# Short outputs as rows through TensorE, silu's slope on ScalarE, and a pool for the spectra products, in a training step of a state-space block with a gated feed-forward layer

## The chip, the cores and the metric

The kernel runs on one core of one Trainium2 chip. The metric is the device time of one execution, in microseconds (us). A core has several engines, each with its own stream of instructions: TensorE (PE in the profile; its weight loads are PEld), VectorE (DVE), ScalarE (ACT), GpSimd (POOL) and SyncE (SP, which here only issues DMA transfers; SPq is its queue). The kernel before took between 934 and 946 us in the median, depending on the group of runs, and in one group its single runs lay between 936.66 and 947.21. So kernels of different groups are compared by their ratio to the kernel before of the same group, or by the length of a stage within one trace.

## The reference, cut to what matters

The reference is a forward pass and its gradient; the outputs are the result and the gradients of the eleven inputs that it depends on. Sizes: L = 2048 positions, D = 512 channels, N = 128 states, F = 1792 hidden units.

```python
xn = layernorm(x)
# A: state-space block, a long convolution by FFT
dt = exp(log_dt)                              # one number per channel: 512
K  = einsum("dn,dnl,dn->dl", C, exp(dt*A*l), dt*B).real
s  = irfft(rfft(xn) * rfft(K)) + xn * Dskip   # Dskip: 512 numbers
# B: feed-forward layer
h  = xn @ w1
g  = silu(silu(h) @ w2)
return x + s * g
# ... and the gradients of x, A, B, C, log_dt, Dskip, w1, w2 for a given grad_out
```

Three parts of the gradient matter here: the gradient of `Dskip` (512 numbers, called ddb in the kernel), the gradient of `log_dt` (512 numbers, ddt), and silu'(h), a factor on every element of the hidden layer's gradient (1792 x 2048), called the slope.

## The kernel before

The kernel interleaves its parts with Python generators, and a scheduler in the compiler places instructions on the engines. It has five stages by time: forward pass, convolution stages (four channel blocks of 128; each does forward and inverse transforms as matmuls), the w2 gradient, the hidden gradient (called the dh stage), and a tail (the last w1-gradient blocks, sixteen tiles of dx, and the parameter gradients of the state-space block).

The gradient of Dskip, once for each channel block. The accumulation leaves one number in each of 128 partitions, and it is stored from there:

```python
ds = C.io.tile([P, T, P], BF16, name="ds_b", tag="ds")
nc.sync.dma_start(ds[:], k.cat_d[:, :, 2, blk])
psd = k.psum1.tile([P, P], F32, name="ps_dsk", tag="psd")
for t in range(T):
    nc.tensor.matmul(out=psd[:], lhsT=ds[:, t, :], rhs=k.xn[:, t, blk], ...)
...scalar_tensor_tensor(out=dd, in0=psd, in1=k.ident, ..., accum_out=dda)
nc.vector.tensor_copy(out=ddb[:], in_=dda[:])                  # 128 partitions x 1
nc.gpsimd.dma_start(k.outs[9][blk].rearrange("(p o) -> p o", o=1), ddb[:])
```

The slope. The forward pass stores silu(h) and tanh(h/2); the backward pass builds the slope from both with two VectorE operations per tile of 128 x 2048 (there are 14):

```python
nc.scalar.activation(out=aT[:, ft, :], in_=pf, func=ACT.Silu)          # forward
nc.scalar.activation(out=th[:, s], in_=pf, func=ACT.Tanh, scale=0.5)
# ... backward, gen_dh, for each tile ft:
nc.vector.tensor_scalar(out=th, in0=th, scalar1=-0.5, scalar2=0.5, ...)
nc.vector.scalar_tensor_tensor(out=th, in0=a, scalar=-1.0, in1=th, op0=ALU.add, op1=ALU.mult)
for tcn in range(4):
    ...   # 4 matmuls into ps_da
    nc.vector.scalar_tensor_tensor(out=k.dhT[:, ft, ls], in0=th[:, ls], scalar=1.0, in1=ps, ...)
# then, for the tile before: DH = transposes of dhT (PE), copied out of PSUM by ScalarE;
# ps_w1 += DH^T xn (16 matmuls), the w1 gradient
```

A small addition on POOL inside the loop that builds the convolution kernel K. It adds Dskip to 32 elements of KF. SP's queue stores KF to K_b right after it, and other transfers stand behind that store in the same queue:

```python
nc.gpsimd.tensor_tensor(out=KF[64*e:64*e+1, 0, :], in0=KF[64*e:64*e+1, 0, :], in1=k.dsk0[...], op=ALU.add)
...
nc.sync.dma_start(K_b[...], KF[...])
```

The end of the parameter gradients, a chain on VectorE (`gen_ssm_final`, run beside the dx tiles; ScalarE only scales two of the outputs).

```python
def emit(out_ap, src, m):
    ob = fin.tile(shp, BF16, name="emit_o", tag="emit_o" + sfx, bufs=2)
    ...                                    # scale into ob
    nc.sync.dma_start(out_ap[bs]..., ob[:])
... # 38 operations on 128 x 512 elements; six results leave through emit
tmul(nc, ddt_b[:], ddt[:], dtb[:])                              # 128 partitions x 4
nc.sync.dma_start(k.outs[8][bs].rearrange("(k p) -> p k", p=P), ddt_b[:])
```

## Time and profile before

Before takes 937.39 us (median; 935.88 to 937.6). Its profiled run has a span of 932.0 us. Stage ends are read from the first and last starts of named matmuls.

| stage of the profiled run | from, to | us |
|---|---|---|
| forward pass | start to last ps_o | 217.7 |
| convolution stages | to first pt_o | 403.5 |
| w2 gradient | to first ps_da | 56.9 |
| dh stage | first to last ps_da | 171.1 |
| tail | last ps_da to end | 82.8 |

The page of before: its first part gives busy time, the second cuts the span into 40 slices of 23.3 us. A digit is the busy share in tenths; PEclk is the clock granted to TensorE, in tenths; GB/s is what the DMA engines moved.

```profile
PE 743.2 (80%) x6870; PEld 488.3 (52%) x6940; DVE 707.4 (76%) x1146; ACT 640.7 (69%) x1174; POOL 95.3 (10%) x147
...
PE   4479899886758887796579668898999797898992
...
PEclk9788999999879999998899979999999898999997
...
GB/s 281 188 135 220 207 255 212 186 238 149 155 66 103 77 230 69 81 125 141 75 81 121 131 178 154 250 210 301 231 258 248 229 255 240 214 239 94 162 84 79
```

No engine is busy throughout. In the slices around 260, 360, 455 and 530 us PE falls to 5 to 7 tenths, in the first three of them with traffic of 66 to 81 GB/s. The table by stretches shows the first of these places. Its columns are the stretch, its length, busy time with instruction count for each of PE, PEld, DVE, ACT and POOL, then PEclk, the DMA share and GB/s:

```profile
247.00:252.00 5.00, 4.95 (x44) 3.02 (x43) 1.85 (x3) 5.00 (x11) 0.69 (x1) 1.00 1.50 113
252.00:256.00 4.00, 3.47 (x63) 2.75 (x61) 3.45 (x7) 3.99 (x10) 0.00 (x0) 1.00 0.91 13
...
260.00:268.00 8.00, 0.48 (x3) 0.30 (x3) 0.40 (x1) 0.52 (x1) 0.00 (x0) 0.67 0.81 59
268.00:272.00 4.00, 3.23 (x20) 2.35 (x21) 1.76 (x4) 2.88 (x5) 0.00 (x0) 0.50 0.57 163
```

At 247 us the Dskip store is issued. Traffic then falls to 13 GB/s, and from 260 to 268 us all engines stand: PE does 0.48 us of work in 8. Afterwards PE runs at half clock. The DMA engines' time is taken (share 0.91 and 0.81), yet few bytes move (13 and 59 GB/s). The view of the tile ddb gives the store itself, with its four issues and the time from issue to landing:

```profile
L728 POOL DMA_DIRECT2D out_dram<-ddb x4: 542/557/689, 247.1 to 520.2; - x4
...
DMA to landing us min/median/max: 15.4/15.4/15.4
```

The waits of PE (line and tile, what released it, us in total, times, longest; "issue" means that the profile names no releaser):

```profile
PE ps_s_3149 L87 <- ACT dftA L74: 12.8, 1, 12.8
PE ps_s_7860 L87 <- ACT KF L74: 9.3, 1, 9.3
...
PE pf_t L619 <- issue: 8.2, 2, 8.0
PE pf_t L619 <- ACT DX L74: 8.0, 1, 8.0
...
PE ps_dsk L721 <- DMA ds_b<-cat_d: 7.1, 3, 6.0
```

The first line is the place at 224 to 237 us. PE's stands after the first, third and fourth Dskip store are the lines with 8.0 (issue), 8.0 (DX) and 9.3 us (KF). In the first ScalarE stood 8.8 us as well, without a named releaser.

In the dh stage VectorE's slope operations are these (view of the tile th_ft; shortest, median and longest in ns):

```profile
L838 DVE TENSOR_SCALAR th_ft<-th_ft x14: 680/685/696, 622.3 to 845.4; 128x2048 bf16<-128x2048 bf16 x14
L839 DVE SCALAR_TENSOR_TENSOR th_ft<-a_ft,th_ft x14: 2278/2292/2293, 623.5 to 846.1; 128x2048 bf16<-128x2048 bf16 x14
```

They cost 14 x (0.685 + 2.292) = 41.7 us of VectorE. In that stage VectorE is busy for 151.0 and PE for 151.0 of 171.1 us. The tail, in three stretches: the last w1 blocks, the dx tiles on PE, and the end after them:

```profile
849.20:861.10 11.90, 9.59 (x69) 5.20 (x70) 2.84 (x6) 6.42 (x8) 11.90 (x21) 1.00 0.55 162
861.10:914.10 53.00, 51.91 (x240) 23.50 (x243) 44.82 (x89) 18.71 (x38) 6.57 (x12) 1.00 0.60 126
914.10:932.00 17.90, 0.40 (x2) 0.00 (x0) 12.78 (x30) 7.63 (x14) 0.00 (x0) 0.61 0.16 59
```

Here PE goes straight on from the last ps_da, and VectorE's parameter chain runs beside the dx tiles.

### The profile page before, as it was taken

The page shows a single profiled execution, that of the slowest core. Times are in us where ns is not written, and L with a number is a line of the kernel's source. Part 1 is how long each engine was busy: PE and PEld are TensorE (multiplying, and loading weights), DVE is VectorE, ACT ScalarE, POOL GpSimd, SP SyncE. Part 2 cuts the span into 40 slices and gives each one's busy share as a digit, 9 for nine tenths or more (in the row PEclk, how much of TensorE's full clock was granted, in tenths as well). Part 3 has the DMA queues.
Part 4 walks back from the last instruction along what each step waited for, and adds up shares of the span by engine and source line. Part 5 has one row for each costly group of instructions (what it writes and reads, how often), then busy time and mean ns, then how long its engine had stood idle before and what let it go on. Part 6 is the DMA issues. An engine that isn't in the chain of part 4 may idle for free. (4 is left out here: it accounts for less than half of the span.)

```text
span 932.0 us, 17458 instructions
## 1 busy us (share of the span) xinstructions
PE 743.2 (80%) x6870; PEld 488.3 (52%) x6940; DVE 707.4 (76%) x1146; ACT 640.7 (69%) x1174; POOL 95.3 (10%) x147
## 2 busy tenths in 40 slices
PE   4479899886758887796579668898999797898992
PEld 1235555554536776684469546564545453544441
DVE  6958899959547988995689238953379898796887
ACT  5998979785858898997699666666635454554144
POOL 4101000304000000021000030010100000006100
PEclk9788999999879999998899979999999898999997
DMA  9436686664953299247934995889898888673562
GB/s 281 188 135 220 207 255 212 186 238 149 155 66 103 77 230 69 81 125 141 75 81 121 131 178 154 250 210 301 231 258 248 229 255 240 214 239 94 162 84 79
DMA packets 194642, 161.97 MB, mean 174 GB/s; under 512 B 132800, under 2 KB 159296, under 8 KB 194560
## 3 DMA queue, kind: packets, MB, share of 16 engines
q1 hardware_dynamic: 189824, 146.43, 61.5%
q0 software_dynamic: 4736, 14.43, 5.5%
q8 instruction: 54, 0.88, 0.4%
q14 instruction: 28, 0.23, 0.1%
HBM read 87.30 MB, written 67.11 MB: 166 GB/s over the span
## 5 line engine op out<-in xcount | busy, mean ns | idle before, releaser
L597 DVE TENSOR_TENSOR ym<-T_97 128x1024 bf16<-128x1024 bf16 x128 | 83.3, 682 | 32.5 <-PE pf_y L636 23.8
L74 ACT CAST Vb<-psV 128x512 bf16<-128x512 f32 x128 | 69.4, 609 | 38.1 <-issue 20.7
L597 DVE TENSOR_TENSOR X<-T_97 128x1024 bf16<-128x1024 bf16 x128 | 81.8, 686 | 14.4 <-PE ps_k L643 14.4
L619 PE MATMUL pf_t<-ident_bfloat_79,X 128*128 128x128 bf16 x1024 | 71.1, 228 | 25.0 <-issue 8.2
L619 PEld LDWEIGHTS <-X 128*128 128x128 bf16 x1024 | 65.6, 103 | 32.0 <-issue 27.5
L74 ACT CAST XTf<-pf_t 128x512 bf16<-128x512 f32 x128 | 67.8, 628 | 1.6 <-PE pf_t L619 1.5
L131 PEld LDWEIGHTS <-prod 128*128 128x128 bf16 x512 | 48.9, 100 | 25.7 <-DVE prod L122 13.8
L678 PE MATMUL ps_h<-XNT,W_127 128*128 128x512 bf16 x213 | 56.9, 407 | 5.9 <-ACT th L682 4.9
L844 PE MATMUL ps_da<-DOT,W2T 128*128 128x512 bf16 x218 | 51.9, 380 | 0.2
L926 PE MATMUL psV<-XT,Gbd 128*128 128x256 bf16 x256 | 42.3, 287 | 11.7 <-ACT Vb L74 5.8
L886 PE MATMUL ps_dx<-W1T,dhT 128*128 128x512 bf16 x220 | 50.6, 379 | 1.1 <-ACT dxn L890 0.9
L692 PE MATMUL ps_o<-W_129,aT 128*128 128x512 bf16 x212 | 50.3, 381 | 1.4 <-ACT th_2090 L696 0.4
L652 POOL TENSOR_TENSOR KF<-KF,dsk_714 1x32 bf16<-1x32 bf16 x16 | 33.3, 2081 | 166.7 <-ACT KF L74 107.4
L926 PEld LDWEIGHTS <-Gbd 128*128 128x128 bf16 x256 | 35.0, 175 | 20.2 <-issue 10.1
L72 DVE COPY dftB<-pt_b 128x1024 bf16<-128x1024 bf16 x24 | 16.5, 687 | 38.1 <-PE pt_b L95 30.1
L87 PEld LDWEIGHTS <-TF 128*128 128x128 bf16 x384 | 26.4, 103 | 31.4 <-issue 21.8
L95 PE MATMUL pt_b<-ident_bfloat_79,dftA 128*128 128x128 bf16 x384 | 30.2, 237 | 15.3 <-ACT dftA L74 7.5
L682 ACT ACTIVATE th<-ps_h 128x512 bf16<-128x512 f32 x56 | 38.0, 685 | 4.2 <-DMA th_d<-th 4.2
L678 PEld LDWEIGHTS <-W_127 128*128 128x128 bf16 x224 | 22.4, 103 | 31.3 <-issue 13.0
L681 ACT ACTIVATE aT<-ps_h 128x512 bf16<-128x512 f32 x56 | 37.9, 681 | 0.2
L643 PEld LDWEIGHTS <-X 128*128 128x128 bf16 x1024 | 35.1, 99 | 5.5 <-issue 2.2
L845 DVE SCALAR_TENSOR_TENSOR dhT<-th_ft,ps_da 128x512 bf16<-128x512 bf16 x56 | 35.2, 679 | 3.0 <-PE ps_da L844 2.9
(1394 smaller groups left out, 1981.2 us busy)
## 6 DMA issues: line engine op xcount, KB each, us to landing
xt_d<-XTf SPq DMA_DIRECT2D x32, 512.0 KB, 2.8
XT<-xt_d SPq DMA_DIRECT2D x32, 512.0 KB, 5.4
YT<-yt_d SPq DMA_DIRECT2D x64, 256.0 KB, 4.0
yt_d<-YTf SPq DMA_DIRECT2D x32, 256.0 KB, 3.4
th_d<-th SPq DMA_DIRECT2D x28, 256.0 KB, 2.3
at_d<-aT SPq DMA_DIRECT2D x4, 1792.0 KB, 6.8
a_ft<-at_d SPq DMA_DIRECT2D x14, 512.0 KB, 6.6
th_ft<-th_d SPq DMA_DIRECT2D x14, 512.0 KB, 6.2
```

The costliest lines, as they stand in the source:

```text
L74: self.nc.scalar.copy(out=out, in_=in_)
L131: nc.tensor.matmul(out=ps[:, gi].rearrange("p a b -> p (a b)"), lhsT=prods[g0 // H][:, ca, cb, g0 % H + gi, :], rhs=W[:, w].rearrange("p a ...
L597: nc.vector.tensor_tensor(out=out.rearrange("p (r h l u) -> p r h l u", h=nh, l=4, u=2), in0=h, in1=l, op=ALU.mult)
L619: nc.tensor.matmul(out=pf[:, qi, m // 2, :], lhsT=X[:, m, q + qi], rhs=k.ident[:], start=(m % 2 == 0), stop=(m % 2 == 1))
L678: nc.tensor.matmul(out=ps[:], lhsT=W1[:, dk, ft * P:(ft + 1) * P], rhs=XNT[:, dk, 4 * tcn:4 * tcn + 4, :], start=(dk == 0), stop=(dk == DK ...
L681: nc.scalar.activation(out=aT[:, ft, :], in_=pf, func=ACT.Silu)
L682: nc.scalar.activation(out=th[:, s], in_=pf, func=ACT.Tanh, scale=0.5)
L692: nc.tensor.matmul(out=pso[:], lhsT=aT[:, ft, tt * P:(tt + 1) * P], rhs=W2[:, ft, :], start=(ft == 0), stop=(ft == FT - 1))
L844: nc.tensor.matmul(out=ps[:], lhsT=W2T[:, dk, rows], rhs=DOT[:, dk, ls], start=(dk == 0), stop=(dk == DK - 1))
L845: nc.vector.scalar_tensor_tensor(out=k.dhT[:, ft, ls], in0=th[:, ls], scalar=1.0, in1=ps[:], op0=ALU.add, op1=ALU.mult)
L886: nc.tensor.matmul(out=ps[:], lhsT=k.dhT[:, ft, t * P:(t + 1) * P], rhs=W1T[:, ft, :], start=(ft == 0), stop=False)
L926: nc.tensor.matmul(out=psV[:, qi].rearrange("p a b -> p (a b)"), lhsT=Gbd[:, :, :, :, 32 * (q_ // 2 % 2) + 4 * c + 2 * (q_ % 2) + q_ // 4] ...
```

## The change

The change has three intents. Short outputs shall leave as contiguous rows and not as one element per partition: TensorE turns them, for Dskip by a matmul with a column of ones, for ddt by a transpose. The slope shall come from ScalarE's own function on stored h. And the spectra products, with the tiles dKs and DXC, shall have a pool of their own, so that they do not share memory with the transforms. Beside these, the chain in the tail takes exp(log_dt) from the forward pass and no longer loads and exponentiates it again.

```diff
-        pr = big.tile([P, 2, 2, H, P], BF16, name="prod", tag="prod", bufs=2)
+        pr = C.pr.tile([P, 2, 2, H, P], BF16, name="prod", tag="prod", bufs=2)
 ...  # dKs and DXC likewise: C.big -> C.pr
-                nc.scalar.activation(out=th[:, s], in_=pf, func=ACT.Tanh, scale=0.5)
-            nc.sync.dma_start(thv[:, f0:f0 + 2, ls], th[:])
+                nc.scalar.copy(out=h_[:, s], in_=pf)
+            nc.sync.dma_start(hv[:, f0:f0 + 2, ls], h_[:])
 ...  # gen_conv_d
-    ...scalar_tensor_tensor(out=dd[:], in0=psd[:], ..., in1=k.ident[:], accum_out=dda[:])
-    ddb = C.io.tile([P, 1], BF16, name="ddb", tag="ddb")
-        nc.gpsimd.dma_start(k.outs[9][blk].rearrange("(p o) -> p o", o=1), ddb[:])
+    nc.vector.tensor_tensor(out=dd[:], in0=psd[:, 0], in1=k.ident[:], op=ALU.mult)
     yield from dft_fwd(k, C, ds[:], DX)
+    nc.tensor.matmul(out=psd[0:1, 1], lhsT=k.ones[:], rhs=dd[:], start=True, stop=True)
+    ddb = C.io.tile([1, P], BF16, name="ddb", tag="ddb")
+    nc.gpsimd.dma_start(k.outs[9][blk].rearrange("(o p) -> o p", o=1), ddb[:])
 ...  # backward
+def silu_slope(k, ft):
+    sl = fa.tile([P, 2048], BF16, name="slope", tag="slope", bufs=3)
+    nc.sync.dma_start(sl[:], k.h_d[ft * P:ft * P + P, :])
+    nc.scalar.activation(out=sl[:], in_=sl[:], func=ACT.Derivative_silu)
 ...  # da(ft): the two VectorE operations go; the last multiply stays
-            nc.vector.scalar_tensor_tensor(out=k.dhT[:, ft, ls], in0=th[:, ls], scalar=1.0, in1=ps[:], ...)
+            nc.vector.tensor_tensor(out=k.dhT[:, ft, ls], in0=sl[:, ls], in1=ps[:], op=ALU.mult)
+        if ft + 2 < FT:
+            silu_slope(k, ft + 2)
 ...  # gen_ssm_final
-        nc.gpsimd.dma_start(ldt[:], k.ins["A_log_dt"][bs].rearrange("(k p) -> p k", p=P))
-    nc.scalar.activation(out=dtb[:], in_=ldt[:], func=ACT.Exp)
+    nc.vector.tensor_copy(out=dtb[:], in_=k.dtN[:, b0:b0 + nb])
 ...
-        nc.sync.dma_start(k.outs[8][bs].rearrange("(k p) -> p k", p=P), ddt_b[:])
+    nc.tensor.transpose(out=pt[0:DK, :], in_=ddt_b[:], identity=k.ident[:])
+    nc.vector.tensor_copy(out=row[:], in_=pt[0:DK, :])
+    nc.sync.dma_start(k.outs[8][bs].rearrange("(k p) -> k p", p=P), row[:])
```

More of the change, by code (lines that the diff above doesn't have):

```diff
@@ L178 @@
     k.at_d = dr.tile([F, L], BF16, name="at_d")
-    k.th_d = dr.tile([F, L], BF16, name="th_d")
+    k.h_d = dr.tile([F, L], BF16, name="h_d")
     k.ident = make_identity(nc, k.const)
@@ L218 @@
         st_fp.close()
-    C = KCtx(); C.big = st_c.enter_context(pool("cbig", "right")); C.io = st_c.enter_context(pool("cio", "right"))
+    C = KCtx(); C.big = st_c.enter_context(pool("cbig", "right")); C.pr = st_c.enter_context(pool("cprod", "right")); C.io = st_c.enter_context(pool("cio", "right"))
     def conv(b):
@@ L488, in ssm_magnitudes @@
         nc.tensor.matmul(out=pd[:, b:b + 1], lhsT=k.dtb[0:1, b * P:(b + 1) * P], rhs=k.ones[0:1, :], start=True, stop=True)
-    dtN = tp.tile([P, NB], F32, name="dtN")
+    dtN = k.dtN = k.const.tile([P, NB], F32, name="dtN")
     nc.vector.tensor_copy(out=dtN[:], in_=pd[:])
@@ L666, in gen_ffn_fwd @@
     W1, XNT, W2 = k.W1, k.XNT, k.W2
-    thv = k.th_d[:].rearrange("(f p) l -> p f l", p=P)
+    hv = k.h_d[:].rearrange("(f p) l -> p f l", p=P)
     atv = k.at_d[:].rearrange("(f p) l -> p f l", p=P)
@@ L672, in gen_ffn_fwd @@
         for f0 in range(0, FT, 2):
-            th = fp.tile([P, 2, 512], BF16, name="th", tag="th", bufs=2)
+            h_ = fp.tile([P, 2, 512], BF16, name="h_", tag="h_", bufs=2)
             for s in range(2):
@@ L717, in gen_conv_d @@
     C.DX = DX = C.big.tile([P, 2, 16, P], BF16, name="DX", tag="DX")
-    psd = k.psum1.tile([P, P], F32, name="ps_dsk", tag="psd")
+    psd = k.psum1.tile([P, 2, P], F32, name="ps_dsk", tag="psd")
     for t in range(T):
-        nc.tensor.matmul(out=psd[:], lhsT=ds[:, t, :], rhs=k.xn[:, t, blk], start=(t == 0), stop=(t == T - 1))
-    dd = C.io.tile([P, P], F32, name="dd", tag="dd")
-    dda = C.io.tile([P, 1], F32, name="dda", tag="dda")
-    nc.vector.scalar_tensor_tensor(out=dd[:], in0=psd[:], scalar=1.0, in1=k.ident[:], op0=ALU.mult, op1=ALU.mult, accum_out=dda[:])
-    ddb = C.io.tile([P, 1], BF16, name="ddb", tag="ddb")
-    nc.vector.tensor_copy(out=ddb[:], in_=dda[:])
-    with nc.allow_non_contiguous_dma(reason="256 B"):
-        nc.gpsimd.dma_start(k.outs[9][blk].rearrange("(p o) -> p o", o=1), ddb[:])
-    yield from dft_fwd(k, C, ds[:], DX)
-    dKs = C.big.tile([P, T, P], BF16, name="dKs", tag="so")
+        nc.tensor.matmul(out=psd[:, 0], lhsT=ds[:, t, :], rhs=k.xn[:, t, blk], start=(t == 0), stop=(t == T - 1))
+    dd = C.io.tile([P, P], BF16, name="dd", tag="dd")
+    nc.vector.tensor_tensor(out=dd[:], in0=psd[:, 0], in1=k.ident[:], op=ALU.mult)
+    yield from dft_fwd(k, C, ds[:], DX)
+    nc.tensor.matmul(out=psd[0:1, 1], lhsT=k.ones[:], rhs=dd[:], start=True, stop=True)
+    ddb = C.io.tile([1, P], BF16, name="ddb", tag="ddb")
+    nc.vector.tensor_copy(out=ddb[:], in_=psd[0:1, 1])
+    nc.gpsimd.dma_start(k.outs[9][blk].rearrange("(o p) -> o p", o=1), ddb[:])
+    dKs = C.pr.tile([P, T, P], BF16, name="dKs", tag="so")
     yield from dft_inv_mul(k, C, C.UX[:], DX[:], dKs, conj_a=True, four=False)
@@ L760, in gen_conv_dx @@
 def gen_conv_dx(k, C, b):
-    DXC = C.big.tile([P, T, P], BF16, name="DXC", tag="so")
+    DXC = C.pr.tile([P, T, P], BF16, name="DXC", tag="so")
     yield from dft_inv_mul(k, C, C.KX[:], C.DX[:], DXC, conj_a=True, four=False)
@@ L797, in gen_dw2 @@
         yield
-def da_loads(k, ft):
+def silu_slope(k, ft):
     nc, fa = k.nc, k.fa
-    rows = slice(ft * P, ft * P + P)
-    a = fa.tile([P, 2048], BF16, name="a_ft", tag="a_ft", bufs=2)
-    nc.sync.dma_start(a[:], k.at_d[rows, :])
-    th = fa.tile([P, 2048], BF16, name="th_ft", tag="th_ft", bufs=2)
-    nc.sync.dma_start(th[:], k.th_d[rows, :])
-    k.aths[ft] = a, th
+    sl = fa.tile([P, 2048], BF16, name="slope", tag="slope", bufs=3)
+    nc.sync.dma_start(sl[:], k.h_d[ft * P:ft * P + P, :])
+    nc.scalar.activation(out=sl[:], in_=sl[:], func=ACT.Derivative_silu)
+    k.slopes[ft] = sl
 def dh_operands(k):
     nc, fa = k.nc, k.fa
-    k.aths = {}
+    k.slopes = {}
     for ft in range(2):
-        da_loads(k, ft)
+        silu_slope(k, ft)
     k.W2T = fa.tile([P, k.DK, k.F], BF16, name="W2T")
@@ L834, in da @@
         rows = slice(ft * P, ft * P + P)
-        if ft not in k.aths:
-            da_loads(k, ft)
-        a, th = k.aths[ft]
-        nc.vector.tensor_scalar(out=th[:], in0=th[:], scalar1=-0.5, scalar2=0.5, op0=ALU.mult, op1=ALU.add)
-        nc.vector.scalar_tensor_tensor(out=th[:], in0=a[:], scalar=-1.0, in1=th[:], op0=ALU.add, op1=ALU.mult)
+        sl = k.slopes.pop(ft)
         for tcn in range(4):
@@ L844, in da @@
                 nc.tensor.matmul(out=ps[:], lhsT=W2T[:, dk, rows], rhs=DOT[:, dk, ls], start=(dk == 0), stop=(dk == DK - 1))
-            nc.vector.scalar_tensor_tensor(out=k.dhT[:, ft, ls], in0=th[:, ls], scalar=1.0, in1=ps[:], op0=ALU.add, op1=ALU.mult)
+            nc.vector.tensor_tensor(out=k.dhT[:, ft, ls], in0=sl[:, ls], in1=ps[:], op=ALU.mult)
+        if ft + 2 < FT:
+            silu_slope(k, ft + 2)
     da(0)
@@ L961, in gen_ssm_final @@
         nc.gpsimd.dma_start(Pm[nm][:], k.ins[key][bs].rearrange("(k p) n -> p k n", p=P))
-    ldt = fin.tile([P, DK], BF16, name="n_ldt" + sfx)
-    with nc.allow_non_contiguous_dma(reason="1 KB"):
-        nc.gpsimd.dma_start(ldt[:], k.ins["A_log_dt"][bs].rearrange("(k p) -> p k", p=P))
     dtb = fin.tile([P, DK], BF16, name="n_dtb" + sfx)
-    nc.scalar.activation(out=dtb[:], in_=ldt[:], func=ACT.Exp)
+    nc.vector.tensor_copy(out=dtb[:], in_=k.dtN[:, b0:b0 + nb])
     ndt = fin.tile([P, DK], BF16, name="n_ndt" + sfx)
@@ L1024, in gen_ssm_final @@
     tmul(nc, ddt_b[:], ddt[:], dtb[:])
-    with nc.allow_non_contiguous_dma(reason="1 KB"):
-        nc.sync.dma_start(k.outs[8][bs].rearrange("(k p) -> p k", p=P), ddt_b[:])
+    pt = k.psumT.tile([P, P], BF16, name="pt_dt", tag="pt")
+    nc.tensor.transpose(out=pt[0:DK, :], in_=ddt_b[:], identity=k.ident[:])
+    row = fin.tile([DK, P], BF16, name="ddt_r" + sfx)
+    nc.vector.tensor_copy(out=row[:], in_=pt[0:DK, :])
+    nc.sync.dma_start(k.outs[8][bs].rearrange("(k p) -> k p", p=P), row[:])
 _INS = ['A_u', 'A_A_re', 'A_A_im', 'A_B_re', 'A_B_im', 'A_C_re', 'A_C_im', 'A_log_dt', 'A_Dskip', 'B_x', 'B_w1', 'B_w2', 'grad_out']
```

## The prediction

> **What bounds it now.** No single engine: the page gives PE 80%, DVE 76%, ACT 69% of 932 us. Time is lost where all stand still.
>
> 1. *Two-byte stores.* Four times (247, 348, 438, 520 us) the Dskip gradient leaves as 128 packets of 2 bytes, 15.4 us to landing each (DMA view). In the table by stretches traffic falls from about 240 to 6-30 GB/s for 12-15 us after each. Other stores queue behind, XTf/YTf buffers stay occupied, and PE, DVE and ACT all stop: 8, 2, 7 and 9 us, with the clock at 0.5 for about 4 us after the long ones: 30 us together. The fifth (893 us) is the 15.3 us DMA entry in the chain of waits, but costs DVE only 4 us of waits. The Trainium skill (DMA: Bandwidth & Descriptors, Rules for kernel authors) says a non-contiguous last dimension becomes one descriptor per element; the trace agrees.
> 2. At 224-237 us PE waits 12.8 us, behind an ACT wait for the last cat_d store, whose memory dftA reuses.
> 3. In the dh stage (680-850 us) PE and DVE are both near full; PE visibly waits only about 14 us.
>
> **What the change does.**
>
> - *Rows:* remove the stalls of point 1: 30 us, less about 7 given back to the next limit (256-byte loads; POOL's KF add, which holds K_b stores): -23 (-12 to -30).
> - *Pool:* in the instruction order dftA no longer waits for a DMA, but ps_dsk needs ds_b, which comes behind the same POOL add (11.6 us): 0 (+/-4).
> - *Forward:* 56 Tanh (0.68 us) become copies (0.6-0.69 us): 0.
> - *Slope:* DVE loses 14 x (0.68 + 2.29) = 42 us; the last multiply stays at 0.68. ACT gains 14 x 1.9 = 27 us (estimate from the skill, ScalarE: Activation LUTs, What ACT_TABLE_LOAD costs: 186 ns + 0.833 ns per element). PE was almost full: -5; the first two slopes delay ACT's DOT copies: +2.
> - *Tail, the cost:* turning ddt puts a transpose on PE. In the changed order it stands directly after the last ps_da, before the last two dW1 blocks and all 16 dx tiles, and waits for DVE's whole parameter-gradient chain: loads about 6 us, then 31 operations of 0.6 us, 18 us. PE stands about 27 us. Then 11.6 us of dW1, about 2 us of slow clock and 16 x 3.24 = 52 us of dx follow in series. From the last ps_da to the end: 82 us before, about 98 after, although the log_dt load (DVE waits 9.1 us) and the 2-byte store are gone: +16 (+10 to +20).
>
> Sum -10: **928 us, range 911 to 944.** Faster by over 2%: 0.21; within 2%: 0.76; slower: 0.03.
>
> **What would show it.** ddb stores landing in about 2 us with no all-engine gap after; conv stages (220-560 us) some 20 us shorter. DVE busy down 40 us, ACT up 25. A PE wait of 20-30 us before the transpose pt_dt, for DVE's ddt_b, with PE near 0 in that slice; dx tiles then paced by PE at 3.24 us, not DVE at 2.5.
>
> **What would make it wrong.** The conv stage may be held by POOL's add, starved by a busier DVE: half the gain. ACT's slopes, in order before PSUM copies, may stall PE more than I count. The parameter chain may finish sooner, the tail cheaper by 5-8 us; with all 30 us of the stores the result would be faster by over 2%.

The DMA view has 32 packets of the first store's queue at 248 to 249 us in before, and 32 for the row at 258 to 259 us in after: the trace does not show one packet per element there. For ddt's store it does (528 packets of the queue between 893 and 896 us, for 512 elements).

## The result, and the profile after

After takes 931.77 us (median; 931.23 to 934.74) against 937.39. The ratio is 0.995, with a 95% interval of 0.9927 to 0.9973: half a per cent faster. Executions over 1.5% slower than the fastest of the same kernel are left out of the means. Ratios in this document are the mean time of one kernel's fast runs over that of the other's in the same rounds, so they are not quite the ratio of the medians quoted. By stage, in the profiled runs:

| stage | before | after | difference | predicted |
|---|---|---|---|---|
| forward pass | 217.7 | 216.8 | -0.9 | 0 |
| convolution stages | 403.5 | 378.9 | -24.6 | -23 |
| w2 gradient | 56.9 | 55.5 | -1.4 | +2 |
| dh stage | 171.1 | 173.4 | +2.3 | -5 |
| tail | 82.8 | 105.4 | +22.6 | +16 |

These two runs differ by 2.0 us in all, the medians by 5.6 us; the stages of one trace are not better than a few us against each other. (The first stage alone took 216.8 to 221.3 us in kernels that share its code.) The page of after:

```profile
PE 736.0 (79%) x6878; PEld 484.8 (52%) x6945; DVE 670.7 (72%) x1116; ACT 666.4 (72%) x1187; POOL 98.4 (11%) x146
...
PE   4469989887488887986798788999798879840997
...
PEclk9889999999698999998999899999899999985999
...
GB/s 279 191 135 225 208 254 219 187 235 143 158 99 103 113 176 63 116 94 180 83 56 227 200 135 238 200 307 215 201 219 200 222 193 208 148 100 127 23 125 45
```

VectorE lost 36.7 us of work and ScalarE gained 25.7, about as forecast. The convolution slices of PE (the 10th to the 25th) hold 7 to 9 tenths but for two: a 4 at 232 to 256 us, which is a wait told below, and a 6. In the tail a slice with PE at 0 has appeared; the slice before it has 4. Nothing like it is in before.

The store of the Dskip gradient, and the stretches after its first issue at 257 us:

```profile
L729 POOL DMA_DIRECT2D out_dram<-ddb x4: 522/523/642, 257.0 to 515.1; - x4
...
DMA to landing us min/median/max: 1.7/2.3/2.6
```

```profile
257.00:262.00 5.00, 4.72 (x81) 4.25 (x78) 4.98 (x8) 4.96 (x11) 0.64 (x1) 1.00 0.42 94
...
266.00:270.00 4.00, 1.83 (x20) 0.97 (x18) 4.00 (x6) 4.00 (x10) 0.00 (x0) 1.00 0.20 68
270.00:278.00 8.00, 6.94 (x105) 6.30 (x104) 8.00 (x14) 6.37 (x14) 0.00 (x0) 1.00 0.30 100
```

The same store lands in 2.3 us, and the standstill is gone: PE does 6.94 us of work in the 8 us from 270, at full clock. (From 266 to 270 it has 1.83 of 4 us, but VectorE and ScalarE are busy throughout.) The waits of PE after:

```profile
PE pt_dt L1020 <- DVE ddt_b L60: 33.5, 1, 33.5
PE ps_dsk L721 <- DMA ds_b<-cat_d: 21.7, 3, 15.2
...
PE ps_w L851 <- ACT DH L74: 10.5, 7, 5.5
```

The first line is the tail's loss: one wait of 33.5 us before the new transpose. The second is the loss that the pool's removal of the dftA wait turned into: PE now waits for ds_b. The third belongs to the dh stage. The tail in stretches:

```profile
824.60:858.50 33.90, 0.38 (x2) 0.00 (x0) 25.92 (x41) 1.25 (x2) 13.94 (x25) 0.55 0.50 143
858.50:871.30 12.80, 10.72 (x68) 6.08 (x71) 0.21 (x1) 4.93 (x6) 0.00 (x0) 0.86 0.00 0
871.30:923.10 51.80, 51.59 (x241) 23.50 (x243) 32.80 (x75) 23.67 (x47) 2.88 (x5) 1.00 0.25 82
923.10:930.00 6.90, 0.36 (x2) 0.00 (x0) 2.62 (x6) 1.50 (x3) 0.00 (x0) 0.77 0.10 38
```

A stretch of 33.9 us with 0.38 us of PE work is new. The w1 blocks take 0.9 us more, the dx tiles 1.2 us less. The end after the last dx matmul is 11.0 us shorter, since the chain is over by then. Together: 33.9 + 0.9 - 1.2 - 11.0 = 22.6. The Trainium skill (TensorE: Matmul & The Clock Gate, Step-by-step: what each phase is for) says that only weight loads are pulled ahead and that the "MATMULs themselves stay in program order". The trace agrees: nothing of the ready w1 blocks ran in the 33.5 us. What the wait consists of shows in VectorE's timeline (start, length, instruction, and in brackets the idle time before it):

```profile
827.74 0.69 DVE L60 TENSOR_TENSOR dBr<-n_Br,n_dtb 128x512 f32<-128x512 bf16 x1 [2.03 <-DMA n_Br<-in_A_B_re_dram]
...
847.43 0.69 DVE L60 TENSOR_TENSOR emit_o<-CSi,n_ndt 128x512 bf16<-128x512 f32 x1 [4.76 <-DMA out_dram<-emit_o]
...
856.85 0.69 DVE L1014 TENSOR_TENSOR ddt_acc<-ddt_acc,cm 128x512 f32<-128x512 f32 x1
857.57 0.69 DVE L1016 TENSOR_REDUCE ddt<-ddt_acc 128x4 f32<-128x512 f32 x1
858.29 0.16 DVE L60 TENSOR_TENSOR ddt_b<-ddt,n_dtb 128x4 bf16<-128x4 f32 x1
```

From dBr to ddt_b are 39 operations, 38 steps from start to start. (858.29 - 827.74 - 4.76) / 38 = 0.68 us each; an operation that needs the one just before it starts 0.72 us after it. In the middle VectorE stands 4.76 us for an output buffer whose store has not landed.

ScalarE's timeline at the beginning of the dh stage, and the load of the slope (view of its tile):

```profile
663.57 1.91 ACT L805 ACTIVATE slope<-slope 128x2048 bf16<-128x2048 bf16 x1 [2.08 <-DMA slope<-h_d]
665.38 1.91 ACT L74 COPY DH<-pt_f 128x1024 bf16<-128x1024 bf16 x2
667.21 1.91 ACT L805 ACTIVATE slope<-slope 128x2048 bf16<-128x2048 bf16 x1
```

```profile
L804 SPq DMA_DIRECT2D slope<-h_d x14: 320/380/1181, 588.4 to 793.8; - x14
L805 ACT ACTIVATE slope<-slope x14: 1909/1914/1968, 596.4 to 800.7; 128x2048 bf16<-128x2048 bf16 x14
...
  DMA slope<-h_d: 7.5, 5
```

The activation takes 1.91 us, which the Trainium skill (ScalarE: Activation LUTs, What ACT_TABLE_LOAD costs) gives as 186 ns + 0.833 ns per element, an estimate of 1.89 us for 2048. But ScalarE stood 2.08 us for its load, then did the slope, and only then the copy DH that PE needed: this is PE's single wait of 5.5 us (2.08 for the load, 1.91 for the slope, the rest for the copy). In all ScalarE waited 7.5 us in five places for these loads.

### The profile page after: what moved, and what is told of

It reads as the page before. It is cut to its first block, busy times and chain, and to the rows that moved or that the text cites. A ratio compares the mean times of both kernels' runs of the same rounds, so it can differ in the third digit from the quotient of the medians.

```text
span 930.0 us, 17456 instructions
## 1 busy us (share of the span) xinstructions
PE 736.0 (79%) x6878; PEld 484.8 (52%) x6945; DVE 670.7 (72%) x1116; ACT 666.4 (72%) x1187; POOL 98.4 (11%) x146
## 5 line engine op out<-in xcount | busy, mean ns | idle before, releaser
L60 DVE TENSOR_TENSOR T<-Vb,YT 128x1024 bf16<-128x1024 bf16 (+1 forms) x96 | 78.1, 863 | 44.6 <-ACT Vb L74 43.5
L597 DVE TENSOR_TENSOR ym<-T 128x1024 bf16<-128x1024 bf16 x128 | 83.6, 682 | 27.7 <-PE pf_y L636 19.3
L597 DVE TENSOR_TENSOR X<-T 128x1024 bf16<-128x1024 bf16 x128 | 81.9, 686 | 5.9 <-PE ps_k L643 5.8
L619 PE MATMUL pf_t<-ident_bfloat,X 128*128 128x128 bf16 x1024 | 69.4, 225 | 10.8 <-ACT h__2430 L682 2.9
L131 PE MATMUL ps_i<-WI,prod 128*128 128x256 bf16 x512 | 64.5, 278 | 15.1 <-DVE prod L122 11.8
L840 DVE TENSOR_TENSOR dhT<-slope,ps_da 128x512 bf16<-128x512 bf16 x56 | 36.6, 683 | 46.0 <-PE ps_da L839 45.8
L74 ACT CAST dftA<-ps_i 128x512 bf16<-128x512 f32 x88 | 48.0, 613 | 22.6 <-PE ps_i L131 22.1
L851 PE MATMUL ps_w<-xn,DH 128*128 128x512 bf16 x211 | 54.9, 405 | 11.2 <-ACT DH L74 10.5
L678 PE MATMUL ps_h<-XNT,W 128*128 128x512 bf16 x213 | 55.4, 397 | 7.2 <-ACT h__633 L682 2.1
L692 PE MATMUL ps_o<-W,aT 128*128 128x512 bf16 x212 | 50.0, 379 | 1.5 <-ACT th L696 0.4
L793 PE MATMUL ps_w<-DO_all,A_ft 128*128 128x512 bf16 x214 | 50.1, 379 | 0.7 <-ACT Vb L74 0.2
L74 ACT CAST dftA<-ps_s 128x512 bf16<-128x512 f32 x92 | 48.6, 670 | 0.1
L95 PE MATMUL pt_b<-ident_bfloat,dftA 128*128 128x128 bf16 x384 | 31.6, 242 | 14.2 <-ACT dftA L74 7.6
```

The costliest lines, as they stand in the source:

```text
L60: nc.vector.tensor_tensor(out=out, in0=a, in1=b, op=ALU.mult)
L74: self.nc.scalar.copy(out=out, in_=in_)
L131: nc.tensor.matmul(out=ps[:, gi].rearrange("p a b -> p (a b)"), lhsT=prods[g0 // H][:, ca, cb, g0 % H + gi, :], rhs=W[:, w].rearrange("p a ...
L597: nc.vector.tensor_tensor(out=out.rearrange("p (r h l u) -> p r h l u", h=nh, l=4, u=2), in0=h, in1=l, op=ALU.mult)
L619: nc.tensor.matmul(out=pf[:, qi, m // 2, :], lhsT=X[:, m, q + qi], rhs=k.ident[:], start=(m % 2 == 0), stop=(m % 2 == 1))
L678: nc.tensor.matmul(out=ps[:], lhsT=W1[:, dk, ft * P:(ft + 1) * P], rhs=XNT[:, dk, 4 * tcn:4 * tcn + 4, :], start=(dk == 0), stop=(dk == DK ...
```

## The experiments

Sixteen kernels ran in five groups. Two of them give wrong results; all the others were correct. Each is told with its ratio to the kernel before of its group; after's own ratio is 0.995.

### a_late: the transpose after the dx tiles

```diff
-    (the transpose, the copy and the store of ddt in gen_ssm_final)
+    (the same three, after interleave([gen_dx(k), gst], [1, 3]); ddt_b lies in the constant pool)
```

> The kernel after, with only the PE transpose of ddt moved: it is emitted after the last dx tile, nothing else changes. Theory (the time lost in the tail is PE standing in program order before the transpose, 33.5 us in the trace of after): PE starts the last dW1 blocks at once after the last ps_da, the stretch from the last ps_da to the end falls from 105.0 to about 75 to 82 us, and the whole to about 904 us (900 to 910). Rival (the tail is bound by VectorE's longer chain and the dx adds behind it, so that PE's wait is only where it shows): the tail stays within 8 us of 105 and the time above 922 us.

Measured: 908.3 us, ratio 0.9611 (0.9549 to 0.9673). In this group before took 946.12, more than in the first, so the expected 904 is missed by 4 us while the ratio is 3.4% below after's. The tail is 77.7 us:

```profile
831.10:843.00 11.90, 9.59 (x69) 5.22 (x70) 8.73 (x14) 4.93 (x6) 11.86 (x21) 1.00 0.55 155
843.00:896.00 53.00, 51.72 (x240) 23.52 (x243) 43.06 (x92) 20.70 (x42) 4.99 (x9) 1.00 0.42 128
896.00:908.80 12.80, 0.55 (x3) 0.08 (x1) 8.13 (x19) 4.97 (x10) 0.00 (x0) 0.62 0.16 58
```

The first two stretches are as long as those of before. What follows: one matmul's place in PE's order cost 105.4 - 77.7 = 27.7 us. The rest of the change in the tail (a row, no second load of log_dt) gains 82.8 - 77.7 = 5.1 us, as far as single traces tell. The rival, that VectorE's chain bound the tail, falls.

### a_ddtcol: ddt as a column again

```diff
-    nc.tensor.transpose(...); copy; nc.sync.dma_start(k.outs[8][bs]...("(k p) -> k p"), row[:])
+    nc.sync.dma_start(k.outs[8][bs].rearrange("(k p) -> p k", p=P), ddt_b[:])
```

> The kernel after, with ddt leaving as a column of 2-byte elements again, without a transpose; the rest as after. Theory: PE no longer waits for ddt, so this gains most of what the moved transpose gains: about 908 us (902 to 915); the 2-byte store itself lands in about 15 us but delays little, since few loads are then outstanding. Rival (the 2-byte store at the end cost as much as the transpose does): 920 us or more.

Measured: 911.92 us, ratio 0.9659 (0.9606 to 0.9712); tail 85.2 us. As expected in size. But "delays little" was wrong: PE waited 10.4 us for a DXC_s load, and then ran at a clock of 0.51. That load was issued from POOL's queue at 872.6 us, 1.6 us after this store, and landed only after 21.3 us. In before the chain ends later: the same store goes out at 893.2 us, after the last DXC_s load (887.7), and PE did not wait for it. A column of single elements cost 85.2 - 77.7 = 7.5 us even here; the transpose in its bad place cost more.

### a_ddbcol: only the Dskip gradient as a column again

```diff
-    nc.vector.tensor_tensor(out=dd, in0=psd[:, 0], in1=k.ident); ones matmul; row store
+    scalar_tensor_tensor with accum_out; [P, 1] store, as in the kernel before
```

> The kernel after, with only the Dskip gradient leaving as a column of 2-byte elements again, four times. Theory (these four stores made the standstills in the convolution stages): the all-engine gaps after each store come back, the stretch to the first ps_da grows by about 23 us and the time is about 955 us (950 to 962). Rival (the pool of their own for the products gave the gain in the convolution stages): below 938 us.

Measured: 955.71 us, ratio 1.0125 (1.007 to 1.0181); the convolution stages took 399.8 us against 378.9 in after. The store's landing, and the stretches of the standstill:

```profile
DMA to landing us min/median/max: 18.2/18.2/18.2
```

```profile
262.00:266.00 4.00, 3.67 (x44) 2.66 (x43) 4.00 (x6) 4.00 (x8) 0.00 (x0) 1.00 1.46 22
...
270.00:280.00 10.00, 4.06 (x50) 3.16 (x51) 8.34 (x15) 3.33 (x9) 0.00 (x0) 0.83 0.73 67
```

The stores are slow again, traffic falls to 22 GB/s, and PE loses its time. So the gain in the convolution stages is theirs: 20.9 us by stage, about 1.75% by ratio (some 16 us). That is less than the 23 expected.

The edit also moves the store, since the row is stored only after the transforms. But this column is issued at 258.6 us, later than after's row (257.0), and still stops the engines: the shape does it, not the place. The packet records of the traces show it too. Packets of the hardware queue (q1 on the page) that took over 3 us stand only in the four kernels that store Dskip's gradient as a column (before, b_pool, b_slope and this one: 87 to 113 each, up to 13.3 us, all begun within 20 us after one of the four stores). The other fourteen have none; their longest took 2.7 us.

### a_th: the slope on VectorE again

```diff
-                nc.scalar.copy(out=h_...); slope: load h, Derivative_silu on ScalarE
+                Tanh in the forward pass; the two VectorE operations per tile, as before
```

> The kernel after, with only the slope undone: Tanh stored in the forward pass, two VectorE operations per tile in the backward. Theory (the slope on ScalarE takes 38 us from VectorE, but PE gains nothing, since ScalarE's in-order slopes delay its PSUM copies as much): the stretch from the first to the last ps_da becomes 171 us (from 173.4), VectorE's busy time is about 38 us more, and the time is within 6 us of the kernel after (926 to 938 us). Rival (the slope gains about 5 us as predicted): 936 us or more, with that stretch 5 us or more longer.

Measured: 937.63 us, ratio 0.9918 (0.9859 to 0.9976), no difference from after within the intervals. The dh stage took 170.5 us, VectorE 709.3 us in all (38.6 more). So far the theory holds: the slope on ScalarE gains nothing as it stands.

### b_pool, b_ddbrow, b_slope: each part alone on the kernel before

```diff
 b_pool:    C.big.tile -> C.pr.tile for prod, dKs, DXC
 b_ddbrow:  the Dskip gradient as a row
 b_slope:   stored h, Derivative_silu on ScalarE
```

> The kernel before, with only the pool of their own for the spectra products. Theory (the pool removes PE's 12.8 us wait for dftA at 224 to 237 us, but ds_b arrives as late, so that PE waits there instead, by about as much): within 4 us of before, and the wait for dftA gone from the waits, with one of 8 to 12 us before ps_dsk in its place. Rival (the pool gives a good part of the gain in the convolution stages): 10 us or more faster.

Measured: 928.23 us, ratio 0.9966 (0.9899 to 1.0032): the same. PE's wait of 12.8 us for dftA is gone. In its place this one (waits of PE) grew from 7.1 us in before, by more than the 8 to 12 us that I expected:

```profile
PE ps_dsk L721 <- DMA ds_b<-cat_d: 22.4, 3, 15.7
```

The convolution stages took 397.4 us, 6.1 less than before; the interval of the ratio leaves room for a gain of 1% or none.

> The kernel before, with only the Dskip gradient leaving as a row. Theory (the 2-byte stores made the four standstills): the stretch from the last ps_o to the first pt_o is 20 to 26 us shorter than before's 403.5 us, the time 20 to 26 us less. Rival (the gain needs the pool as well, or comes from it): less than 12 us.

Measured: 906.14 us, ratio 0.9706 (0.9674 to 0.9739): 27.8 us less between medians. The convolution stages took 377.5 us, 26.0 less than before; the store lands in 2.1 us. This one part alone is faster than the whole change.

> The kernel before, with only the slope from ScalarE on stored h. Theory (VectorE is relieved of 42 us but PE is not faster, as ScalarE's slopes stand in order before its PSUM copies and wait for their own loads): the stretch from first to last ps_da is 171 to 176 us (before 171.1), ScalarE busier by 26 us, VectorE less by 38, the time within 5 us of before. Rival (the slope gains 5 us, as I predicted): that stretch below 167 us and the time 4 us or more below before.

Measured: 939.39 us, ratio 1.0057 (1.0015 to 1.0098): slower by half a per cent. Dh stage 173.8 us, ScalarE 27.2 us busier, VectorE 38.8 less. The rival, my forecast, falls.

### a_kfdve: the KF add on VectorE

```diff
-            nc.gpsimd.tensor_tensor(out=KF[64 * e:64 * e + 1, 0, :], ...)
+            nc.vector.tensor_tensor(out=KF[64 * e:64 * e + 1, 0, :], ...)
```

> The kernel after, with the small KF add on VectorE instead of POOL. Theory (the next limit in the convolution stages is that add: it took up to 14.86 us on POOL while VectorE was busy, and held the K_b store, and with it the ds_b load, for which PE stood 21.7 us in three waits): the ds_b waits fall below 8 us in sum and the stretch from the last ps_o to the first pt_o falls from 379 by 10 to 20 us. Rival (the add's wait is only where other bandwidth or PE work is covered): less than 5 us.

Measured: 907.97 us, ratio 0.9724 (0.9703 to 0.9744), 2.3% below after. The convolution stages took 360.1 us (18.8 less), and the ds_b waits fell from 21.7 to 3.7 us. (The forward pass, where the first of these adds stand, took 212.5 us, against 216.8 to 221.3 in the kernels with the add on POOL.) In after the add is this (view of KF; shortest, median, longest):

```profile
L652 POOL TENSOR_TENSOR KF<-KF,dsk x16: 234/402/14860, 119.9 to 513.3; 1x32 bf16<-1x32 bf16 x16
```

and in this run:

```profile
L652 DVE TENSOR_TENSOR KF<-KF,dsk x16: 155/166/168, 122.4 to 488.4; 1x32 bf16<-1x32 bf16 x16
```

An addition of 32 elements took up to 14.86 us on POOL while VectorE was busy. SP's queue issued nothing from 219.7 to 234.6 us, since the store of KF came next in it; the ds_b load was issued at 240.0. The Trainium skill (SBUF — State Buffer, SBUF: two separate sides) describes a port pair that VectorE and GpSimd share as "an exclusive lock": whichever holds it keeps it for its whole instruction (of VectorE's operations, those with two inputs in SBUF are among the ones that use it). The 14.86 us against 0.23 fit that, but they span several VectorE instructions; no run here shows how the turns are given.

### a_pre: the slope's loads one tile earlier

```diff
-    sl = fa.tile(..., tag="slope", bufs=3); load and activation together
+    sl = k.raw.pop(ft); slope_load(k, ft + 1)   # a fourth buffer; the activation follows as before
```

> The kernel after, with each slope's load issued one tile earlier into a fourth buffer; the activation stays where it was. Theory A (the dh stage lost its gain because ScalarE, in order, stands 7.5 us for the slope's load and holds the DH copies behind it, on which PE waits 9.5 us): ScalarE's waits for the load fall below 1.5 us, PE's waits for DH in the dh stage to 2 to 4 us, and the stretch from first to last ps_da from 173.4 to 167 to 170 us. Theory B (it is the 1.9 us that each slope itself takes in ScalarE's order, not its load): the load waits vanish, but PE's waits for DH stay above 6 us and the stretch at 172 us or more.

Measured: 933.19 us, ratio 0.9922 (0.9895 to 0.9949). The dh stage took 169.9 us, in the range of theory A. PE waited 5.9 us for DH (9.5 in after). But ScalarE's waits for the loads stayed at 7.0 us: the scheduler moved the activations too, so one more slope was done before the dh stage, and the first DH copy came ahead of the waiting slope. The edit did not do what it was meant to, and cannot decide between A and B. It suggests that a wait for a load costs PE less when no copy that PE needs stands behind it.

### a_emit: six output buffers in the tail

```diff
-        ob = fin.tile(shp, BF16, name="emit_o", tag="emit_o" + sfx, bufs=2)
+        ob = fin.tile(shp, BF16, name="emit_o", tag="emit_o" + sfx, bufs=6)
```

> The kernel after, with six buffers in place of two for the parameter gradients that VectorE sends out in the tail, so that it waits for none of these stores. Theory (4.8 us of PE's 33.5 us wait for ddt were VectorE waiting for one of these stores to land, a term I had left out): PE's wait falls to about 28.7 us, the stretch from the last ps_da to the end from 105.4 to about 100.6, the time by 4 to 5 us. Rival (VectorE meets another wait right after, or the four large loads that delayed the store delay the chain's inputs): less than 2 us.

Measured: 932.3 us, ratio 0.9903 (0.9882 to 0.9925), an interval just below that of after. The tail took 101.5 us (3.9 less), and VectorE waited for no store. PE's wait:

```profile
PE pt_dt L1020 <- DVE ddt_b L60: 29.0, 1, 29.0
```

So 4.5 us of the 33.5 were the wait for a buffer. The rest is the chain itself and its first loads.

### a_noact and a_noload: the slope taken apart (wrong results on purpose)

```diff
 a_noact:   the load stays, the activation is left out
 a_noload:  no load; the activation reads k.xn[:, 0:4, :], which lies in the on-chip memory
```

> The kernel after with no slope at all: stored h is loaded and multiplied as it is (wrong results on purpose). VectorE keeps its relief and ScalarE gets no new work. Theory (the relief of VectorE is worth about 2 to 4 us to PE, and ScalarE's slopes cost 3 to 6): stretch from first to last ps_da 166 to 169 us, against 173.2 to 174.0 in the runs with the slope on ScalarE and 170.0 to 171.1 in those with it on VectorE; PE's wait for DH about 2 us. Rival (VectorE's work was never in PE's way, and the relief is worth nothing): 170 us or more.

> The kernel after with the slope activation reading xn, which lies in the on-chip memory, in place of loaded h (wrong results on purpose): ScalarE's work is the same, only the load is gone. Theory A (the load waits of 7.5 us make the loss): the stretch from first to last ps_da falls to 168 to 170.5 us, and PE's waits for DH to 2 to 5 us. Theory B (the 1.9 us of each slope in ScalarE's order make it): the stretch stays at 172 us or more and PE's waits for DH above 6 us.

Measured: a_noact 927.12 us, ratio 0.9822 (0.9764 to 0.9879), dh stage 164.7 us; a_noload 930.71 us, ratio 0.9866 (0.9818 to 0.9913), dh stage 165.8 us. Both stages came out shorter than expected (166 to 169, and 168 to 170.5 for theory A). PE's wait for DH was 2.9 us in both, against 9.5 in the dh stage of after. For a_noload (waits of PE in its dh stage):

```profile
PE ps_w L850 <- ACT DH L74: 2.9, 3, 1.6
```

The first ps_da came 2 us later in these runs relative to the stage before, so the sum of the w2 and dh stages is the safer measure:

| | slope | w2 + dh stages, us |
|---|---|---|
| before | VectorE | 228.0 |
| a_noact | none | 222.2 |
| a_noload | ScalarE, no load | 222.9 |
| after | ScalarE, with load | 228.9 |

VectorE's relief is worth 5.8 us, slightly more than I had forecast. The fourteen activations take back 0.7, although each lasts 1.91 us. The load takes back 6.0. It is not the load's traffic, since a_noact has the loads too. Theory B falls: neither the work alone nor the load alone was the trouble, but ScalarE's wait for the load before copies that PE needs.

Two things limit these figures. They are single traces: the five kernels with the slope on VectorE lie between 226.1 (b_ddbrow) and 228.6 (a_th), the seven with after's slope between 227.2 (a_kfdve) and 230.2 (a_ddtcol). So the relief is 3.9 to 6.4 us, the load's part 4.3 to 7.3, and the 0.7 is within the scatter. And the scheduler orders ScalarE slightly differently in each of these kernels: a_pre still waited 7.0 us for loads, but with a DH copy ahead of the slope, and stands at 226.0. So about half of the 6.0 goes with the order.

### a_poolq and best_poolq: the loads from POOL's queue

```diff
-    nc.sync.dma_start(sl[:], k.h_d[ft * P:ft * P + P, :])
+    nc.gpsimd.dma_start(sl[:], k.h_d[ft * P:ft * P + P, :])
```

> The kernel after, with the slope's loads issued from POOL's queue instead of SP's, where they stand behind state loads that wait for their buffers; a correct kernel. Theory (the load wait makes the loss, and the load is late because of its place in SP's queue): ScalarE's waits for the load fall below 2 us in the stage from first to last ps_da, PE's waits for DH to about 3 us, and the stage to 165 to 168.5 us, close to the 165.8 of the run without the load. Rival (the load is late from the traffic itself, or POOL's queue is held as long): the waits stay above 5 us and the stage at 170 us or more.

Measured: 960.08 us, ratio 1.0275 (1.0229 to 1.0321): a clear miss. The loads got worse (view of the slope tile):

```profile
L804 POOL DMA_DIRECT2D slope<-h_d x14: 527/534/796, 596.0 to 818.5; - x14
...
  DMA slope<-h_d: 36.6, 10
```

ScalarE waited 36.6 us for them; the dh stage took 187.5 us, and w2 and dh stages together 252.6. Waits for the load of 0, 7.5 and 36.6 us go with 222.9, 228.9 and 252.6 us for the two stages. But the larger loss does not come through DH: in the dh stage PE's wait for DH was 10.3 us (9.5 in after), that for wt, another of ScalarE's copies, 8.2 (0.8 in after).

The theory that SP's queue made the loads late falls too. POOL waited 95.1 us in ten places for VectorE to free the slope's buffer before it issued a load, with stores of o10b behind it in the queue. In after it is much the same: seven of the eleven loads from 659 us on were issued within 0.12 us of the end of a multiply of VectorE that reads a slope (681.40 and 681.47 us, for one). So the number of buffers sets when most loads go out. From POOL's queue they then took 6.0 us to land (median; up to 14.2) against 5.3 (up to 6.4). The one run with a buffer more, a_pre, still waited 7.0 us; none has two more.

> The kernel after with three edits: ddt's transpose after the last dx tile, the KF add on VectorE, and the slope's loads on POOL's queue. If the stage from first to last ps_da falls to 165 to 168 us here too, the time is 2 to 4 us below that of the version with the earlier loads (ratio to before 0.9321): a ratio of 0.928 to 0.931. If not, 0.932 to 0.936.

Measured: 905.36 us, ratio 0.9681 (0.9639 to 0.9723); dh stage 190.6 us. Neither branch of the expectation: the stage grew as in a_poolq.

### best_pre and best_th: versions with what the runs showed

```diff
 best_pre:  after + ddt's transpose late + KF add on VectorE + slope loads one tile earlier
 best_th:   after + ddt's transpose late + KF add on VectorE, slope by Tanh on VectorE
```

> The kernel after with three edits together: the ddt transpose after the last dx tile, the KF add on VectorE, and the slope loads one tile earlier. Expected from the single edits, if they add up: 27 us and 20 us below after, and the prefetch 0 to 5 us: about 881 us (874 to 890) where before takes 937. If they get in each other's way (the time gained in the convolution stages returned in the tail): above 895.

> As the run with three edits, but the slope by Tanh and VectorE as before instead of the slope on ScalarE. Theory (the slope on ScalarE gains nothing even when its loads come early): within 3 us of the other, with its stretch from first to last ps_da at 170 us. Rival (with the early loads VectorE's relief pays): 4 us or more slower than the other.

Measured: best_pre 877.37 us, ratio 0.9321 (0.9298 to 0.9343); best_th 879.96 us, ratio 0.9354 (0.9328 to 0.9379). Both beat both kernels by over 5%; the edits add up. The two differ by 2.6 us with intervals that overlap: as far as these runs go, the slope on ScalarE is about even with VectorE, even with earlier loads. (Their w2 and dh stages took 225.9 and 226.4 us.)

## Why the prediction was right or wrong

The forecast was a gain of 10 us, for a time of 928 us with a range of 911 to 944. The gain was 5.6 us between medians, at 931.77. The class and the range held; the size of the gain was about half, and two terms of the sum failed.

- *Rows, -23.* Right in mechanism and size. The convolution stages became 24.6 us shorter; b_ddbrow alone made them 26.0 shorter and the kernel 27.8 us faster; a_ddbcol gave 20.9 us back. That XTf and YTf buffers are what the engines stood for, as the prediction says, stays open: the profile names no releaser for PE's first stand.
- *Pool, 0.* Right within the noise: b_pool was the same, with the wait for dftA turned into one for ds_b. The cause named for it, the KF add on POOL that holds SP's queue, was right too: moving that add (a_kfdve) freed 18.8 us.
- *Forward, 0.* Right, -0.9 us, within the scatter of that stage.
- *"Slope: DVE loses 42 us ... PE was almost full: -5; the first two slopes delay ACT's DOT copies: +2."* This step failed. The two stages together lost 0.9 us in place of gaining 3. The relief itself was sized well (5.8 us, a_noact), and ScalarE's added work is almost free (0.7 us, a_noload). The missing term is the input: when ScalarE's next operation is a slope whose load has not landed, the copies out of PSUM behind it wait as well, and PE waits for those. That cost about 6.0 us between a_noload and after, of which a_pre, with a copy put ahead of a slope, got back 2.9. I had costed the operation and not its operand's arrival, although I wrote that slopes before PSUM copies "may stall PE more than I count".
- *"Tail, the cost: ... PE stands about 27 us ... +16."* Right in mechanism, as a_late shows. The mis-sized term is PE's stand: 33.9 us from last ps_da to the transpose. I took "31 operations of 0.6 us, 18 us"; they are 39, with 38 steps of 0.68 us, 25.8 us. I had no term for the output buffer, 4.76 us in the trace; a_emit, without that wait, shortened PE's stand by 4.5 us. The loads at the beginning, put at 6 us, took about 3. 25.8 + 4.8 + 3 = 33.6. (My own items, 6 and 18, come to 24; the text does not say where the other 3 of the 27 come from.)

The errors: 6.6 us in the tail and 3.9 us in the slope, both towards slower, against 1.6 us more gain from the rows than forecast and 0.9 us in the forward pass. They sum to the 8 us by which the profiled pair (2.0 us of gain) missed the forecast; between medians the miss was 931.77 - 928 = 3.8 us.

## What to carry to other kernels

When work is moved to an idle engine, ask what waits behind it in that engine's order, and when its operand lands: here fourteen operations of 1.9 us cost next to nothing without their loads (0.7 us, within the scatter) and about 6.7 us with them. A tiny instruction that depends on a long chain belongs at the end of TensorE's program; the same transpose cost 27.7 us in one place and nothing visible in another. Stores with one small element per partition are worth a turn to a row even when few bytes are involved, because what they delay is the other traffic; and when such a stall is removed, look for the next holder of the same queue (here a 32-element add).

## What the Trainium skill lacked or had wrong

- DMA: Bandwidth & Descriptors (Rules for kernel authors) says that a strided or non-contiguous last dimension lowers to one descriptor per element, but gives no time. Here 128 elements of 2 bytes landed in 15.4 us (18.2 in a_ddbcol), packets of the hardware queue took up to 13.3 us (at most 2.7 in the kernels without such a store), traffic fell to 13 to 22 GB/s, and all engines stood up to 8 us. As a row of 256 bytes it landed in 2.3 us.
- SBUF — State Buffer (SBUF: two separate sides) describes the lock between VectorE and GpSimd for the length of an instruction. It does not say how long GpSimd can go without a turn: an add of 32 elements took 0.23 us at best and 14.86 us at worst.
- ScalarE: Activation LUTs has no entry for Derivative_silu, as far as I found. It took 1.91 us for 128 x 2048, the rate that the page gives for other functions.
- Vector Engine (DVE) Microarchitecture Reference (5.2 Measured stream behaviour on trn2) gives 1.0417 ns per column plus about 75 ns for back-to-back instructions, an estimate of 0.61 us for 512 elements, and independent operations here start 0.61 us apart. An operation that reads the result of the one just before it starts 0.72 us after it; that section gives no figure for this, and a chain of 39 such and other operations ran at 0.68 us from start to start.
